# Attention, then two mixtures of experts: attention's row-max scaling and tail on other engines, weight splits placed among attention's units, acc scalings spread over product groups

## The chip, the cores and the metric

The kernel runs on one core of a Trainium2 chip. The metric is the device time of one execution in microseconds (us), lower is better. PE is the tensor engine, DVE the vector engine, ACT the scalar engine, POOL the GpSimd engine; SP only issues DMAs here. Each engine runs its own instructions strictly in order, and waits on semaphores for the others.

## The reference, cut to what matters

Sizes are B = 4, H = 8, S = 576, D = 64; N = B*S = 2304 tokens of DM = 512; E = 8 experts of hidden width F = 1024.

```
scores = where(mask, scale * q @ k.T, -1e9)     # window of 32 back; in heads 4 to 7 every 4th position
attn   = exp(scores - scores.max(-1)); attn /= attn.sum(-1) + 1e-9
x      = (attn @ v).transpose(0, 2, 1, 3).reshape(N, DM)

# first mixture: every token goes to one expert, 288 tokens at most each, best gate logits first
out[tokens of e] = relu(x[tokens of e] @ w1[e]) @ w2[e]

# second mixture: on the output of the first
P = exp(logits - logits.max())
for _ in range(8):
    P /= P.sum(1) + 1e-9;  P /= P.sum(0) + 1e-9;  P *= N / E
out = sum over e of P[:, e] * (relu(x @ w1[e]) @ w2[e])
```

## The kernel before, in words

**Attention** (L105 to L335) cuts the four batches into 25 units (`NU`), most of 96 queries of both kinds of heads (plain and dilated), and runs a software pipeline over n = 0 to 27: in step n PE makes the scores of unit n (mask and k.q products, L167, L174), DVE the row maximum (L180) and its scaling by -SC (L181, a tensor_mul of two small SBUF tiles), PE transposes the exponentials of unit n-1 (L197), DVE copies them out of PSUM (L204), ACT makes the 8 exponentials of unit n (L189), and PE multiplies unit n-2 by v (L215), with the gate logits of 128 tokens beside it where these are due (L280). DVE divides by the row sums (`rc`, `xt`, L219 to L221). `x_out` (unit n-3) splits `xt` in a float16 high part (ACT, L232) and a low part (POOL, L234), which SP stores to `xd` in DRAM (L237). The gate logits read `xd` back transposed; for the last batch `x_turn` transposes `xo` on PE (L250) into tiles of its own in PSUM, and ACT copies these into `xl` (L254); the table `TURN` says after which steps. All q and k of batches 1 to 3 are loaded ahead of the loop on SP's queue (L121), ahead of the first store to `xd`.

**Routing.** `Router.phase` (L444 to L572) finds the tokens of one expert in search steps: DVE compares (L476), PE counts (L480), DVE tests (L482), PE spreads the result (L485), DVE narrows (L488 to L490, L468). Phase 0 has nothing else to run beside it; the kernel puts dummy matmuls there (`warm`, L643), and the first six of eight pieces of expert 0's weights of the second mixture's hidden stage: `weights`, with a high half by ACT (L679) and a low half by DVE (L680), 128x1024 each. The last two pieces come in the first mixture's expert 0.

**The mixtures.** The first mixture's products are at L731 and L768, and further ones at L812. In `last()`, the end of stage 1, the Sinkhorn rounds (L1103 to L1143) run beside these as a second stream, a round at each `yield 6000` of the main stream's costs (a planner's nanoseconds); rounds that are left over run in stage 2's first block. In a round DVE divides rows and columns (L1132 to L1142) and PE sums over partitions (L1138). Stage 2 works expert by expert in blocks of tokens: `s_l1` (L995) and `s_l2` (L1033) with seven products each that are combined by additions on ACT and DVE. `add()` (L1057 to L1063) takes a finished product out of PSUM; for e = 1 it first scales two rows of the accumulator `acc` by expert 0's weight P on ACT (L1057, twice), then copies the product (L1058).

Of the kernel before, what the change touches and what calls it, by code (L numbers as in the profile page):

```python
# [16 lines left out]
OP = mybir.AluOpType  # L17
# [66 lines left out]
TURN = {NU - 1: (NU - 7, NU - 6), NU: (NU - 5, NU - 4), NU + 2: (NU - 2, NU - 1)}  # L84
# [22 lines left out]
def attention(tc, q, k, v, masks, wg, ident, xd, L, zero):  # L107

    nc = tc.nc
    with ExitStack() as ctx:  # L110
# [8 lines left out]
        def load_qk(nm, b, kind):  # L119
            x = raw[nm, b, kind] = one.tile([128, 2, S], F32, name="raw%s%d%d" % (nm, kind, b))  # L120
            nc.sync.dma_start(x, src[nm][b, :, 2 * kind:2 * kind + 2])  # L121
# [13 lines left out]
        negc = one.tile([QB, 2, 4], F32)  # L135
        nc.gpsimd.memset(negc, -SC)
# [40 lines left out]
        def row_max(u):  # L177
            p, gs = SS[u], part(u, 4)
            nm = wk.tile([QB, 2, 4], F32, name="nm")
            nc.vector.tensor_reduce(nm[:, :, gs], p[:, :, gs], axis=AX.X, op=OP.max)  # L180
            nc.vector.tensor_mul(nm[:, :, gs], nm[:, :, gs], negc[:, :, gs])  # L181
            PP[u] = nm

        def exps(u):
            p, nm, gs = SS.pop(u), PP[u], part(u, 4)
            e = wk.tile([QB, 2, 4, 128], F32, name="e")
            for s in range(2):
                for g in range(gs.start, gs.stop):
                    nc.scalar.activation(e[:, s, g, :], p[:, s, g, :], AF.Exp, bias=nm[:, s, g:g + 1], scale=SC)  # L189
            PP[u] = e  # L190
# [15 lines left out]
        def pv(u, extra):  # L206
# [4 lines left out]
            hs, ks = part(u, H), part(u, 2)  # L211
            for h in range(hs.start, hs.stop):
# [5 lines left out]
            xt = wk.tile([QB, 2, 4, D], F32, name="xt")  # L218
            nc.vector.tensor_scalar(rc[:, ks], pp[:, ks, :, D:], 1e-9 / SX, None, op0=OP.add)  # L219
            nc.vector.reciprocal(rc[:, ks], rc[:, ks])  # L220
            nc.vector.tensor_mul(xt[:, ks], pp[:, ks, :, :D], rc[:, ks].to_broadcast([QB, ks.stop - ks.start, 4, D]))  # L221
            XT[u] = xt
            for f in fin:
                f()

        def x_out(u):
            xt, ks = XT.pop(u), part(u, 2)
            if u in XO:
                xo = XO[u]
            else:  # L230
                xo = wk.tile([QB, 2, 2, 4, D], F16, name="xo")
# [10 lines left out]
        def x_turn(*units):  # L242

            for u in units:
                p = ps.tile([128, 2, 512], F32, name="ps_s").bitcast(F16)[:, :, :4 * QB].rearrange(
                    "p k (c q) -> p k c q", c=4)
                ks = part(u, 2) if u > (B - 1) * NJ else slice(1, 2)
                for kind in range(ks.start, ks.stop):
                    for c in range(4):
                        nc.tensor.transpose(p[:, kind, c, :], XO[u][:, kind, c // 2, 2 * (c % 2):2 * (c % 2) + 2, :],  # L250
                                            idh)
                for kind in range(ks.start, ks.stop):
                    for o, n, tok, st in tokens_of(QB * UNITS[u][kind][1], QB, kind):
                        nc.scalar.activation(xl[kind][:, :, tok:tok + st * (n - 1) + 1:st], p[:, kind, :, o:o + n],  # L254
                                             AF.Copy)

        XB, XO = {}, {}
# [30 lines left out]
        for b in range(1, B if True else 2):  # L288
            for kind in (1, 0):
                for nm in "kq":  # L290
                    load_qk(nm, b, kind)
            if b == 1:
                for kind in (1, 0):
                    load_v(b, kind)
        nc.scalar.activation(wgh, wgf, AF.Copy, scale=SG)
        nc.vector.scalar_tensor_tensor(wgl, wgf, SG, wgh, op0=OP.mult, op1=OP.subtract)
        xl = [one.tile([128, 4, S], F16, name="xl%d" % kind) for kind in range(2)]
        for n in range(NJ + 1):
            XO[(B - 1) * NJ + n] = one.tile([QB, 2, 2, 4, D], F16, name="xo%d" % n)
        first = S * (B - 1) // 128  # L300
        for n in range(NU + 3):
# [5 lines left out]
            if n < NU:  # L307
                exps(n)
            if n in FILL:
                warm(FILL[n])  # L310
            if n == NU + 1:
                x_turn(NU - 3)
            if 2 <= n <= NU + 1:
                pv(n - 2, [loaded.pop(0)[1] for _ in range(1 if n < NU else 2) if loaded and loaded[0][0] <= n])
# [3 lines left out]
            if n >= 3:  # L318
                x_out(n - 3)
# [9 lines left out]
            x_turn(*TURN.get(n, ()))  # L329
        p = ps.tile([128, 2, 512], F32, name="ps_v", bufs=1)  # L330
        rest = [i for _, i in loaded] + list(range(first, NT))
# [61 lines left out]
class Router:  # L393
# [39 lines left out]
    def start(self, ctx):  # L433
        self.wk = ctx.enter_context(self.tc.tile_pool(name="r_wk", bufs=2))
# [169 lines left out]
class Moe:  # L604
    def __init__(self, ctx, tc, router, xd, ident, w1a, w2a, wg2, w1b, w2b, out, ps, zero):
        nc = self.nc = tc.nc
        self.tc, self.r, self.xd, self.out, self.ps = tc, router, xd, out, ps
# [3 lines left out]
        self.big, self.raw, self.sm = pool("m_big", 1), pool("m_raw", 4), pool("m_s", 1)  # L611
# [3 lines left out]
        self.acc = self.big.tile([128, NT, DM], F32, name="acc")  # L615
# [6 lines left out]
        self.W, self.balanced, self.scattered = {}, False, []  # L622
        self.wb = [[self.big.tile([128, 4, 7, 256], F16, name="w%d%s" % (n, c)) for c in "hl"] for n in (1, 2)]
# [11 lines left out]

    def psum(self):
# [8 lines left out]
    def weights(self, key, letter, fetch, some=slice(None)):  # L645
# [9 lines left out]
        todo = todo[some]  # L655
        live, tiles = [], {lay: t for (k, lay), t in self.W.items() if k == key}
# [13 lines left out]
        for n in range(len(todo)):  # L670
            (lay, k, per, m), r = live.pop(0)
            if lay not in tiles:
                if letter == "a":
                    tiles[lay] = [self.wp.tile([128, (KT, FT)[lay], m], F16, name="w%d%s" % (lay, c)) for c in "hl"]
                else:
                    tiles[lay] = self.wflat[lay]
                self.W[key, lay] = tiles[lay]
# [337 lines left out]
    def s_l2(self, e):  # L1015
# [62 lines left out]
        for q, t, p in order:  # L1078
            yield from prod(q, t, p)
            if p[-1] == every[-1] and q in (2, 6, 4, 3):  # L1080
# [25 lines left out]
    def sinkhorn(self):  # L1106
# [24 lines left out]
        for it in range(8):  # L1131
# [4 lines left out]
            yield 6000  # L1136
# [9 lines left out]
    def stage1(self, ctx):  # L1146

        pool = lambda n, b: ctx.enter_context(self.tc.tile_pool(name=n, bufs=b))
# [13 lines left out]
        for _ in w0:  # L1162
            pass
# [6 lines left out]
        def fetched(ph):  # L1170
            w = self.weights(("a", ph), "b", self.fetch_gather(ph))
# [5 lines left out]
        first = itertools.chain(fetched(0), self.weights(("b", 0), "a", self.fetch_static(0), slice(6, None)))  # L1177

        self.ready = self.direct(1)
        def main():  # L1180
# [10 lines left out]
            for ph in range(E):  # L1191
# [34 lines left out]
        self.warm(16)  # L1226
# [65 lines left out]
def tile_kernel(ctx, tc, q, k, v, wg, w1a, w2a, wg2, w1b, w2b, masks, ident, rtab, thr, out):  # L1292
    nc = tc.nc
    with tc.manual_schedule():
# [5 lines left out]
        attention(tc, q, k, v, masks, wg, ident, xd, L, router.zero)  # L1300
        ps = ctx.enter_context(tc.tile_pool(name="ps", bufs=2, space=bass.MemoryType.PSUM))
        router.ps = ps
        moe = Moe(ctx, tc, router, xd, ident, w1a, w2a, wg2, w1b, w2b, out, ps, router.zero)
        with ExitStack() as stage:
            moe.stage1(stage)
# [21 lines left out]
```

## Time and profile before

| what | value |
|---|---|
| median of 3 runs | 1838.8 us (1835.52 to 1842.16) |
| the profiled execution | 1833.92 us, its span 1832.1 us |
| mean granted clock of PE in it | 0.979 |
| busy share of the span: PE, DVE, ACT, POOL | 96%, 75%, 46%, 12% |

All times of rows are microseconds from the span's start, in that one execution; it lies 4.9 us below the median of the runs. PE's busy share is an average: attention takes 0 to 128 us, phase 0 of the routing to 165 us, the first mixture and the Sinkhorn rounds to 652 us, stage 2 the rest.

### The profile page before, as it was taken

To read this page: it belongs to the slowest core of one execution; us is meant where nothing else is said; L and a number is where in the kernel's file an instruction comes from. 1 tells how busy PE (TensorE), PEld (TensorE's weight loads), DVE (VectorE), ACT (ScalarE), POOL (GpSimd) and SP (SyncE) were. 2 spreads that over 40 slices of the span, in tenths; PEclk is the share of its full clock that TensorE was granted. 3 is DMA by queue.
4 is the path that set the end of the run, shared out by engine and by line. 5 is a ranking of instruction groups with operands and counts; after the bars stand their busy time and mean duration, and the time that the engine had idled before them with its cause. 6 is when DMAs were issued, how large, how long until landed. Compare 5 with 4: busy or idle time off the path is not lost.

```text
span 1832.1 us, 35300 instructions
## 1 busy us (share of the span) xinstructions
PE 1752.7 (96%) x14518; PEld 1297.8 (71%) x14518; DVE 1371.9 (75%) x2625; ACT 839.1 (46%) x1502; POOL 227.4 (12%) x284
## 2 busy tenths in 40 slices
PE   8986899999999889999999999999999999999998
PEld 6873666666677647766777777777777777777776
DVE  5877776686744767877887888788878878887656
ACT  4662333333344344564444555444555444554333
POOL 1224222233221000000000000000000000000111
PEclk8988899999999999999999999999999999999999
DMA  8554323343242314433244432444352353433120
GB/s 304 148 138 138 110 83 95 109 119 104 88 142 83 122 47 156 147 131 146 112 167 164 184 125 105 171 156 152 136 195 93 127 213 140 163 122 141 55 96 35
DMA packets 106161, 241.19 MB, mean 132 GB/s; under 512 B 46704, under 2 KB 70512, under 8 KB 99088
## 3 DMA queue, kind: packets, MB, share of 16 engines
q1 hardware_dynamic: 84736, 151.34, 23.9%
q0 software_dynamic: 20592, 87.53, 13.4%
q8 instruction: 113, 1.85, 0.4%
q14 instruction: 48, 0.39, 0.1%
q10 hardware_dynamic: 672, 0.08, 0.0%
HBM read 173.83 MB, written 61.73 MB: 129 GB/s over the span
## 4 chain that ended last, share of the span: by engine, by line
PE 70%; DVE 11%; issue 10%; ACT 4%; DMA 3%; POOL 1%; SPq 0%; POOLq 0%; ACTq 0%; DVEq 0%
PE mm L995 26%; PE mm L1033 22%; PE mm L731 8%; PE mm L812 5%; PE mm L768 2%; PE ps_v L215 1%; PE r L480 1%; PE ps_p L197 1%; DVE hl L952 1%; PE ps_s L174 1%; POOL out_dram L1047 1%; DVE w1l L680 1%; DMA wgf<-in_wg_dram 1%; DMA rawk<-in_k_dram 1%; DVE G L552 1%
## 5 line engine op out<-in xcount | busy, mean ns | idle before, releaser
L995 PE MATMUL mm<-xb,w1h 128*128 128x384 f16 x2352 | 574.6, 327 | 5.3 <-DVE mm L966 4.9
L1033 PE MATMUL mm<-w2h,hh 128*128 128x256 f16 x1764 | 480.8, 273 | 8.5 <-DVE t L1059 4.4
L1033 PE MATMUL mm<-w2h,hl 128*128 128x256 f16 x1764 | 480.8, 273 | 0.0
L1033 PE MATMUL mm<-w2l,hh 128*128 128x256 f16 x1764 | 480.8, 273 | 0.0
L995 PE MATMUL mm<-xb,w1l 128*128 128x384 f16 x1176 | 383.9, 326 | 0.0
L1033 PEld LDWEIGHTS <-hh 128*128 128x128 f16 x3528 | 345.2, 98 | 52.6 <-issue 10.6
L995 PEld LDWEIGHTS <-w1h 128*128 128x128 f16 x2352 | 230.4, 98 | 159.5 <-issue 11.6
L1033 PEld LDWEIGHTS <-hl 128*128 128x128 f16 x1764 | 172.6, 98 | 20.0
L952 DVE TENSOR_TENSOR hl<-r,hh 128x1536 f16<-128x1536 f32 x84 | 147.5, 1756 | 41.2 <-ACT hh L951 41.2
L995 PEld LDWEIGHTS <-w1l 128*128 128x128 f16 x1176 | 115.2, 98 | 76.5 <-issue 0.7
L947 ACT ACTIVATE r<-mm 128x384 f32<-128x384 f32 x252 | 119.0, 481 | 98.3 <-PE mm L995 98.3
L951 ACT ACTIVATE hh<-r 128x1536 f16<-128x1536 f32 x84 | 124.6, 1483 | 46.4 <-DVE r L976 44.4
L913 POOL DMA_DIRECT2D ws<-raw x48 | 26.0, 541 | 941.1 <-ACT raw L864 673.6
L958 ACT ACTIVATE mm<-mm 128x384 f32<-128x384 f32 x84 | 40.3, 479 | 180.8 <-PE mm L995 180.8
L952 DVE TENSOR_TENSOR hl<-S,hh 128x1152 f16<-128x1152 f32 x84 | 113.6, 1352 | 0.0
L731 PE MATMUL mm<-xt,w1h 128*128 128x288 f16 x512 | 97.2, 289 | 1.4 <-ACT xt L745 1.4
L1043 DVE SCALAR_TENSOR_TENSOR acc<-t,P,acc 128x512 f32<-128x512 f32 x126 | 94.8, 752 | 4.5
L951 ACT ACTIVATE hh<-S 128x1152 f16<-128x1152 f32 x84 | 96.4, 1147 | 0.0
L864 ACT ACTIVATE raw<-raw 128x1024 f16<-128x1024 f32 x48 | 50.6, 1055 | 96.6 <-DVE raw L849 47.7
L734 ACT ACTIVATE w1h<-mm 128x288 f16<-128x288 f32 (+1 forms) x120 | 47.1, 397 | 102.6 <-PE mm L731 100.5
L735 DVE SCALAR_TENSOR_TENSOR w1l<-mm,w1h 128x288 f16<-128x288 f32 (+1 forms) x120 | 50.7, 435 | 55.1 <-ACT w1h L734 54.5
L731 PE MATMUL mm<-x2l,w0h 128*128 128x256 f16 x288 | 81.1, 282 | 6.8 <-DVE x2l L773 6.8
(258 smaller groups left out, 2972.1 us busy)
## 6 DMA issues: line engine op xcount, KB each, us to landing
xb<-xw SPq DMA_DIRECT2D x30, 1344.0 KB, 5.6
ws<-raw POOLq DMA_DIRECT2D x48, 448.0 KB, 2.7
ws<-r POOLq DMA_DIRECT2D x48, 448.0 KB, 3.0
raw<-in_w2b_dram SPq DMA_DIRECT2D x32, 512.0 KB, 9.4
raw<-in_w1b_dram SPq DMA_DIRECT2D x56, 256.0 KB, 6.3
w1h<-ws SPq DMA_DIRECT2D x6, 1792.0 KB, 7.5
w1l<-ws SPq DMA_DIRECT2D x6, 1792.0 KB
w2h<-ws SPq DMA_DIRECT2D x6, 1792.0 KB
```

Of the source, the lines that this page charges most:

```text
L731: nc.tensor.matmul(p, a[:, k, 128 * f:128 * (f + 1)], rhs(k, b), start=(k == 0 and i == 0), stop=(k == KT - 1 and i == 2))
L734: nc.scalar.activation(h[0][:, f, :n], p, AF.Relu)
L735: nc.vector.scalar_tensor_tensor(h[1][:, f, :n], p, 0.0, h[0][:, f, :n], op0=OP.max, op1=OP.subtract)
L812: nc.tensor.matmul(p, a[:, f, c], b[:, f, :], start=(f == 0 and n == 0), stop=(f == FT - 1 and n == 2))
L864: self.nc.scalar.activation(hi[:, k], x, AF.Copy, scale=sw)
L947: nc.scalar.activation(o, p, AF.Relu, scale=SH)
L951: yield nc.scalar.activation(hq[0][:, i, k], x, AF.Copy)
L952: yield V.tensor_sub(hq[1][:, i, k], x, hq[0][:, i, k])
L958: nc.scalar.activation(Q[i], P[i], AF.Copy)
L995: nc.tensor.matmul(p, w[u][:, 2 * j + i // 2, k, 128 * (i % 2):128 * (i % 2 + 1)], x[:, v, r, j], start=(q in (1, 5) and j == 0 and n == 0 ...
L1033: nc.tensor.matmul(p, h[u][:, i, a, 128 * t:128 * (t + 1)], w[v][:, i, b, :], start=(q in (1, 7) and i == 0 and j == 0), stop=(q in (2, 3) ...
L1043: V.scalar_tensor_tensor(self.acc[:, r, :], x, self.P[:, r, e:e + 1], self.acc[:, r, :], op0=OP.mult, op1=OP.add)
```

## The change

1. The scaling of the row maximum goes from DVE to ACT.
2. `exps` is cut in two halves of four exponentials, and `x_out` of unit n-3 stands between them.
3. `x_turn` transposes float32 `xt` (two transposes a kind where there were four) into free columns of the PSUM tile that `pv` uses in the same step, for units 18 to 22 in steps 21 to 25, for 23 and 24 after the loop. The high part is an ACT copy as before, in pieces half as wide; the low part is a DVE subtraction out of PSUM.
4. q and k of batches 2 and 3 are loaded in steps 6, 7, 12 and 13.
5. All eight pieces of expert 0's second-mixture weights are split inside attention: 16 halves of 128x512, one on ACT and the one before on DVE in each of the steps 6 to 23; their loads are issued from step 4 on.
6. Phase 0 has no splits; its `warm` counts go from 5 to 3 per step, and the one ahead of the first mixture from 16 to 6.
7. In `s_l2` for e = 1 the six `acc` scalings stand one after each fourth product group.
8. Sinkhorn's `yield 6000` becomes `yield 4000`: all eight rounds fall into `last()`.

```diff
             nm = wk.tile([QB, 2, 4], F32, name="nm")
             nc.vector.tensor_reduce(nm[:, :, gs], p[:, :, gs], axis=AX.X, op=OP.max)
-            nc.vector.tensor_mul(nm[:, :, gs], nm[:, :, gs], negc[:, :, gs])
+            nc.scalar.activation(nm[:, :, gs], nm[:, :, gs], AF.Copy, scale=-SC)
...
-        def x_turn(*units):
...
+        def x_turn(u, p):
+
+            p = p[:, :, 264:264 + 2 * QB].rearrange("p k (c q) -> p k c q", c=2)
+            ks = part(u, 2) if u > (B - 1) * NJ else slice(1, 2)
+            for kind in range(ks.start, ks.stop):
+                for c in range(2):
+                    nc.tensor.transpose(p[:, kind, c, :], XT[u][:, kind, 2 * c:2 * c + 2, :], idf[:QB, :QB])
...
+            for n, (o, i, x) in enumerate(parts):
+                if x == 0:
+                    nc.scalar.activation(o, i, AF.Copy)
+                else:
+                    nc.vector.tensor_sub(o, i, hi[n - len(hi)])
...
-            if n < NU:
-                exps(n)
+            ex = exps(n) if n < NU else iter(())
+            next(ex, None)
+            if 3 <= n <= NU:
+                x_out(n - 3)
+            for _ in ex:
+                pass
...
+            if 4 <= n:
+                next(side, None)
...
+            b, c = divmod(n - NJ, NJ)
+            if 0 <= b < B - 2 and c < 2:
+                for nm in "kq":
+                    load_qk(nm, b + 2, 1 - c)
...
+    def first_weights(self, ctx):
...
+            for c in (slice(0, 512), slice(512, 1024)):
+                nc.scalar.activation(hi[:, c], r[:, c], AF.Copy, scale=(SW1, SW2)[lay])
+                yield
+                nc.vector.scalar_tensor_tensor(lo[:, c], r[:, c], (SW1, SW2)[lay], hi[:, c], op0=OP.mult,
+                                               op1=OP.subtract)
+                if c.stop == 1024 and n + 4 < len(todo):
+                    load(n + 4)
...
             if q == 2:
-                for r in (row(t, 0), row(t, 1)) if e == 1 else ():
-                    nc.scalar.activation(self.acc[:, r, :], self.acc[:, r, :], AF.Copy, scale=self.P[:, r, 0:1])
...
+            if n % 4 == 3 and rows:
+                r = rows.pop(0)
+                nc.scalar.activation(self.acc[:, r, :], self.acc[:, r, :], AF.Copy, scale=self.P[:, r, 0:1])
...
-            yield 6000
+            yield 4000
...
-            self.warm(1 if need < 2000 else 5)
-            if i % 2 and i < 14:
-                next(w0, None)
+            self.warm(1 if need < 2000 else 3)
...
-        self.warm(16)
+        self.warm(6)
```

First place: DVE in one of attention's steps with gate logits. `nm` is the row maximum, `pt` the transposed exponentials, `xt` the output of a unit, `L` the gate logits; `w0l` is a low half of the weights. Before:

```order
L180 TENSOR_REDUCE nm<-ps_s 96x8
L181 TENSOR_TENSOR nm<-nm,negc 96x8
L204 COPY pt<-ps_p 128x768
L219 TENSOR_SCALAR rc<-ps_v 96x8
L220 RECIPROCAL rc<-rc 96x8
L221 TENSOR_TENSOR xt<-ps_v,rc 96x512
L282 COPY L<-ps_v 128x8
```

and after:

```order
L176 TENSOR_REDUCE nm<-ps_s 96x8
L201 COPY pt<-ps_p 128x768
L218 TENSOR_SCALAR rc<-ps_v 96x8
L219 RECIPROCAL rc<-rc 96x8
L220 TENSOR_TENSOR xt<-ps_v,rc 96x512
L274 COPY L<-ps_v 128x8
L669 SCALAR_TENSOR_TENSOR w0l<-raw,w0h 128x512
```

The scaling is gone from its place behind the maximum, and a split, which reads two SBUF tiles as the scaling did, stands at the step's end, right ahead of the next maximum.

Second place: ACT, and then DVE, in step 23 of the changed kernel, near attention's end. `xl_186` and `xl_187` are the transposed outputs of the last batch, `e` the exponentials, `xo` the high part that is stored.

```order
L177 ACTIVATE nm<-nm 96x8
L186 ACTIVATE e<-ps_s,nm 96x128 x4
L228 ACTIVATE xo<-xt 96x2x256
L186 ACTIVATE e<-ps_s,nm 96x128 x4
L251 ACTIVATE xl_186<-ps_v 128x2x96
L251 ACTIVATE xl_187<-ps_v 128x2x96
```

```order
L176 TENSOR_REDUCE nm<-ps_s 96x8
L201 COPY pt<-ps_p 128x768
L253 TENSOR_TENSOR xl_186<-ps_v,xl_186 128x2x96
L253 TENSOR_TENSOR xl_187<-ps_v,xl_187 128x2x96
L218 TENSOR_SCALAR rc<-ps_v 96x8
L219 RECIPROCAL rc<-rc 96x8
L220 TENSOR_TENSOR xt<-ps_v,rc 96x512
```

Before, these steps held no L253 on DVE and ACT's copies into `xl` stood behind the exponentials of unit 24; now the subtractions stand ahead of the division of the same step, behind ACT's copies, which stand behind all eight exponentials.

Third place: ACT in stage 2's first block with e = 1, behind the hidden layer. `raw` are weights being prepared for the next expert, `t_9009` and its like take the products out of PSUM. Before:

```order
L864 ACTIVATE raw<-raw 128x1024
L864 ACTIVATE raw<-S 128x768
L1057 ACTIVATE acc<-acc,P 128x512 x2
L1058 ACTIVATE t_9033<-mm 128x256
L1057 ACTIVATE acc<-acc,P 128x512 x2
L1058 ACTIVATE t_9037<-mm 128x256
L1057 ACTIVATE acc<-acc,P 128x512 x2
L1058 ACTIVATE t_9041<-mm 128x256
```

and after:

```order
L1115 ACTIVATE acc<-acc,P 128x512 x2
L898 ACTIVATE raw<-raw 128x1024
L898 ACTIVATE raw<-S 128x768
L1115 ACTIVATE acc<-acc,P 128x512 x3
L898 ACTIVATE raw<-raw 128x1024
L898 ACTIVATE raw<-S 128x768
L1115 ACTIVATE acc<-acc,P 128x512
L1090 ACTIVATE t_9009<-mm 128x256
L1090 ACTIVATE t_9013<-mm 128x256
L1090 ACTIVATE t_9017<-mm 128x256
```

All six scalings now stand ahead of the first copy out of PSUM.

## Rows read from the trace of the kernel before

**Rows 1.** The page, busy time and share of the span.

```profile
PE 1752.7 (96%) x14518; PEld 1297.8 (71%) x14518; DVE 1371.9 (75%) x2625; ACT 839.1 (46%) x1502; POOL 227.4 (12%) x284
```

**Rows 2.** Stretches: length, busy PE, PEld, DVE, ACT, POOL; clock, DMA share, GB/s.

```profile
60.00:80.00 20.00, 20.00 (x257) 17.76 (x256) 19.13 (x33) 13.16 (x46) 5.77 (x5) 1.00 0.58 141
...
600.00:640.00 40.00, 34.57 (x278) 25.87 (x275) 30.58 (x86) 14.55 (x34) 0.00 (x0) 0.91 0.38 114
```

**Rows 3.** Timeline of PE, 36 to 56 us: start, duration, instruction, idle before.

```profile
36.92 1.12 PE L174 MATMUL ps_s<-rawk,rawq 64*96 64x128 f32 x16
40.41 2.20 PE L197 MATMUL ps_p<-idf,e 96*128 96x96 f32 x8 [2.37 <-ACT e L189]
...
45.90 2.03 PE L174 MATMUL ps_s<-rawk,rawq 64*96 64x128 f32 x16
...
51.53 1.12 PE L174 MATMUL ps_s<-rawk,rawq 64*96 64x128 f32 x16
...
55.16 1.01 PE L174 MATMUL ps_s<-rawk,rawq 64*96 64x128 f32 x14
```

**Rows 4.** Timeline of ACT: at 39 us, and in a later step.

```profile
39.47 0.63 ACT L232 ACTIVATE xo<-xt 96x512 f16<-96x512 f32 x1 [4.62 <-DMA xd<-xo]
...
106.69 2.15 ACT L189 ACTIVATE e<-ps_s,nm 96x128 f32<-96x128 f32 x8 [1.37 <-DVE nm L181]
```

**Rows 5.** Timeline of DVE: L181 at 54 us, and a step with gate logits.

```profile
53.95 0.16 DVE L181 TENSOR_TENSOR nm<-nm,negc 96x8 f32<-96x8 f32 x1
...
104.50 1.21 DVE L180 TENSOR_REDUCE nm<-ps_s 96x8 f32<-96x1024 f32 x1
105.75 0.83 DVE L181 TENSOR_TENSOR nm<-nm,negc 96x8 f32<-96x8 f32 x1
106.50 0.94 DVE L204 COPY pt<-ps_p 128x768 f32<-128x768 f32 x1
...
108.53 1.21 DVE L180 TENSOR_REDUCE nm<-ps_s 96x8 f32<-96x1024 f32 x1
```

**Rows 6.** Timeline of POOL in the same step.

```profile
105.40 1.15 POOL L234 TENSOR_TENSOR xo<-xt,xo 96x512 f16<-96x512 f32 x1 [2.88 <-ACT xo L232]
```

**Rows 7.** Timeline of DVE: a search step without a split, one with.

```profile
132.39 0.27 DVE L482 TENSOR_SCALAR ok<-r,rem 8x64 f16<-8x64 f32 x1 [0.77 <-PE r L480]
132.94 0.23 DVE L488 TENSOR_SCALAR pen<-r 128x64 f32<-128x64 f32 x1 [0.27 <-PE r L485]
...
139.03 0.24 DVE L482 TENSOR_SCALAR ok<-r,rem 8x32 f16<-8x32 f32 x1 [0.47 <-PE r L480]
139.20 1.20 DVE L680 SCALAR_TENSOR_TENSOR w0l<-raw,w0h 128x1024 f16<-128x1024 f32 x1
140.33 0.17 DVE L488 TENSOR_SCALAR pen<-r 128x32 f32<-128x32 f32 x1
```

**Rows 8.** Timeline of PE ahead of the first mixture.

```profile
165.58 5.62 PE L643 MATMUL mm<-zero 128*128 128x512 f16 x16
```

**Rows 9.** Waits of PE from 610 us to the end: us, times, longest.

```profile
PE mm L995 <- DVE mm L966: 4.9, 3, 2.4
PE mm L1033 <- DVE t L1059: 4.4, 3, 2.7
PE mm L1033 <- DVE t L1063: 4.0, 3, 1.3
```

**Rows 10.** Timeline of ACT in stage 2's first block with e = 1.

```profile
704.83 1.32 ACT L1057 ACTIVATE acc<-acc,P 128x512 f32<-128x512 f32 x2
706.05 0.36 ACT L1058 ACTIVATE t<-mm 128x256 f32<-128x256 f32 x1
```

**Rows 11.** Timeline of DVE between Sinkhorn rounds.

```profile
624.66 2.09 DVE L867 SCALAR_TENSOR_TENSOR w1l<-raw,w1h 128x1024 f16<-128x1024 f32 x2
...
647.05 0.31 DVE L1139 TENSOR_REDUCE cs<-r 128x8 f32<-128x144 f32 x1 [2.43 <-PE r L1138]
...
649.03 0.31 DVE L1135 TENSOR_TENSOR P<-P,rs 128x144 f32<-128x144 f32 x1
```

More of the change, by code (lines that the diff above doesn't have):

```diff
@@ L1 @@
-import itertools
 from contextlib import ExitStack
@@ L104, in lay_v, with attention @@
     return out
-def attention(tc, q, k, v, masks, wg, ident, xd, L, zero):
+def attention(tc, q, k, v, masks, wg, ident, xd, L, zero, side):
     nc = tc.nc
@@ L119, in load_qk @@
         def load_qk(nm, b, kind):
-            x = raw[nm, b, kind] = one.tile([128, 2, S], F32, name="raw%s%d%d" % (nm, kind, b))
+            x = raw[nm, b, kind] = ld.tile([128, 2, S], F32, name="raw%s%d" % (nm, kind))
             nc.sync.dma_start(x, src[nm][b, :, 2 * kind:2 * kind + 2])
@@ L226, in x_out @@
         def x_out(u):
[L227 to L231, printed above, removed]
+            xt, ks = XT[u], part(u, 2)
+            xo = wk.tile([QB, 2, 2, 4, D], F16, name="xo", bufs=4)
             nc.scalar.activation(xo[:, ks, 0], xt[:, ks], AF.Copy)
@@ L240, in x_out @@
                         xo[p0:p0 + n, kind].rearrange("q a h d -> q (a h d)"))
-        def x_turn(*units):
[L244 to L257, printed above, removed]
+        def x_turn(u, p):
[4 more added lines that the diff above has]
+                    nc.tensor.transpose(p[:, kind, c, :], XT[u][:, kind, 2 * c:2 * c + 2, :], idf[:QB, :QB])
+            parts = [(xl[kind][:, x, :, tok:tok + st * (n - 1) + 1:st], p[:, kind, :, o:o + n], x)
+                     for x in range(2) for kind in range(ks.start, ks.stop)
+                     for o, n, tok, st in tokens_of(QB * UNITS[u][kind][1], QB, kind)]
+            hi = [o for o, _, x in parts if x == 0]
+            for n, (o, i, x) in enumerate(parts):
[3 more added lines that the diff above has]
+                    nc.vector.tensor_sub(o, i, hi[n - len(hi)])
+        XB = {}
         def x_load(c, c1):
@@ L287, in attention @@
         loaded = []
[L288 to L294, printed above, removed]
+        for kind in (1, 0):
+            for nm in "kq":
+                load_qk(nm, 1, kind)
+        for kind in (1, 0):
+            load_v(1, kind)
         nc.scalar.activation(wgh, wgf, AF.Copy, scale=SG)
         nc.vector.scalar_tensor_tensor(wgl, wgf, SG, wgh, op0=OP.mult, op1=OP.subtract)
-        xl = [one.tile([128, 4, S], F16, name="xl%d" % kind) for kind in range(2)]
-        for n in range(NJ + 1):
-            XO[(B - 1) * NJ + n] = one.tile([QB, 2, 2, 4, D], F16, name="xo%d" % n)
+        xl = [one.tile([128, 2, 2, S], F16, name="xl%d" % kind) for kind in range(2)]
         first = S * (B - 1) // 128
-        for n in range(NU + 3):
+        for n in range(NU + 2):
             if n < NU:
@@ L328, in attention @@
                 x_load(first, first + 1)
-            x_turn(*TURN.get(n, ()))
+            if n == NU:
+                loaded += [(n, i) for i in (first, first + 1)]
+        x_turn(NU - 2, ps.tile([128, 2, 512], F32, name="ps_s"))
+        x_turn(NU - 1, ps.tile([128, 2, 512], F32, name="ps_p", bufs=1))
+        x_out(NU - 2)
+        x_out(NU - 1)
         p = ps.tile([128, 2, 512], F32, name="ps_v", bufs=1)
-        rest = [i for _, i in loaded] + list(range(first, NT))
+        rest = [i for _, i in loaded] + list(range(first + 2, NT))
         o = p[:, 0, :E * len(rest)].rearrange("p (n e) -> p n e", e=E)
@@ L433, in start @@
     def start(self, ctx):
-        self.wk = ctx.enter_context(self.tc.tile_pool(name="r_wk", bufs=2))
+        self.wk = ctx.enter_context(self.tc.tile_pool(name="r_wk", bufs=2, side="right"))
     def psum(self):
@@ L622, in __init__, with after_attention @@
         self.W, self.balanced, self.scattered = {}, False, []
+    def after_attention(self, ctx):
+        pool = self.tc.tile_pool(name="ps", bufs=2, space=bass.MemoryType.PSUM)
+        self.ps = self.r.ps = ctx.enter_context(pool)
+        self.big = ctx.enter_context(self.tc.tile_pool(name="m_big", bufs=1))
+        self.acc = self.big.tile([128, NT, DM], F32, name="acc")
         self.wb = [[self.big.tile([128, 4, 7, 256], F16, name="w%d%s" % (n, c)) for c in "hl"] for n in (1, 2)]
@@ L654, in weights @@
                 todo.append((lay, k, per, m))
-        todo = todo[some]
-        live, tiles = [], {lay: t for (k, lay), t in self.W.items() if k == key}
+        live, tiles = [], {}
         def load(it):
@@ L672, in weights @@
             if lay not in tiles:
[L673 to L677, printed above, removed]
+                self.W[key, lay] = tiles[lay] = self.wflat[lay]
             hi, lo = (t[:, k:k + per, :] for t in tiles[lay])
@@ L1077, in s_l2 @@
         order += [(q, t, every) for q in (6, 4, 3) for t in ts]
-        for q, t, p in order:
+        rows = [row(t, half) for t in ts for half in range(2)] if e == 1 else []
+        for n, (q, t, p) in enumerate(order):
             yield from prod(q, t, p)
+            if n % 4 == 3 and rows:
+                r = rows.pop(0)
+                nc.scalar.activation(self.acc[:, r, :], self.acc[:, r, :], AF.Copy, scale=self.P[:, r, 0:1])
             if p[-1] == every[-1] and q in (2, 6, 4, 3):
@@ L1175, in fetched @@
             return w
-        first = itertools.chain(fetched(0), self.weights(("b", 0), "a", self.fetch_static(0), slice(6, None)))
+        first = fetched(0)
         self.ready = self.direct(1)
@@ L1299, in tile_kernel @@
         router = Router(ctx, tc, L, rtab, thr, ("r", 2))
[L1300 to L1303, printed above, removed]
+        moe = Moe(ctx, tc, router, xd, ident, w1a, w2a, wg2, w1b, w2b, out, router.zero)
         with ExitStack() as stage:
+            attention(tc, q, k, v, masks, wg, ident, xd, L, router.zero, moe.first_weights(stage))
+            moe.after_attention(ctx)
             moe.stage1(stage)
```

82 lines of the change are left out of this document (46 added, 36 removed).

## The prediction

> **What bounds the kernel now.** I start with the page's busy shares: PE works 96% of the span, every other engine 75% or less [rows 1]. So a saving counts only where PE waits, runs at half clock, or idles behind another engine. The table by stretches shows where that is. Attention's middle has no idle PE, yet DVE is full too, 19.13 of 20 us [rows 2]: a step ends when the slower of the two is through. The Sinkhorn stretch (PE 34.57 of 40, clock 0.91) has slack on PE. Then the timelines of these and of attention's edges.
>
> Early in attention PE stands for 2.37 us on ACT's exponentials, and its next scores take 2.03 us where the same 16 matmuls take 1.12 before and after [rows 3]: TensorE is at its lower level, 1.2 GHz, in place of 2.4. ACT was late because it waited 4.62 us for an earlier store of `xo` [rows 4]; in the code that store stands on SP's queue behind all loads of q and k.
>
> A step late in attention takes 108.53 - 104.50 = 4.03 us, and DVE has not a gap in it. The scaling L181 takes 0.83 us there and 0.16 us elsewhere, for the same 96x8 [rows 5]; in the slow case POOL's subtraction runs from 105.40 to 106.55, and L181 ends 0.03 us after it [rows 6]. A DVE instruction on two SBUF tiles is evidently held while POOL reads. In stage 2 the list of waits leaves 4.9 us on the hidden layer and 4.4 + 4.0 us on products whose PSUM is late [rows 9].
>
> **The change part by part.** The sum is against the profiled execution, 1833.9 us.
>
> Early attention: -7. Two steps take 51.53 - 36.92 = 14.6 us. The next, undisturbed and without gate logits, takes 55.16 - 51.53 = 3.63 [rows 3]. Two such are 7.3, so 7.3 us are lost. With eight q and k loads out of the way and `xo` in four buffers the store is issued earlier, and the halved exponentials don't stand behind it. The weight pieces now loaded at the same time are smaller than what goes. Bounds: -2.4 (only the wait goes, the clock falls anyway) and -7.3.
>
> Steps 7 to 22: +5. DVE loses the 0.75 us from L181's start to the next [rows 5], and gets a split of 512 columns: half of 1.20 us [rows 7], 0.6. Alone that is 3.28 + 0.62 = 3.9 us against 4.03, a gain of 0.1 a step, or 1 to 2 in all. But the split reads two SBUF tiles too. Counted from the maximum's start, DVE comes to it at 4.03 - 0.75 = 3.28 in a step with gate logits, 0.07 earlier without. POOL's subtraction starts after the maximum (1.21), the scaling on ACT (no row; between 0.16, as on DVE [rows 5], and 0.36 for ACT's 256 columns [rows 10]; I take 0.25), half of 2.15 for four exponentials, 0.63 for `xo` [rows 4], and some 0.1 for each of the two hand-overs: 3.3 to 3.4. That is a dead heat. Where POOL is first, the split waits until 3.3 + 1.15 = 4.45 and the step lasts 5.05, 1.0 more than before. Eight of the sixteen steps have gate logits, and in those PE has the logits' matmuls to do ahead of DVE's division, so DVE tends to be late there. Five steps lost is my value; bounds -2 (none) and +10 (eight, and two of the others).
>
> By the Trainium skill ("SBUF — State Buffer", "Who interferes with whom") a DVE instruction with two SBUF inputs contends with a GpSimd instruction that reads SBUF, and the one issued first holds the shared pair while the other fully blocks. The trace's 0.16 against 0.83 agrees. By it, the steps cost nothing if the split is always issued first and the total would be 5 to 7 lower; POOL first everywhere would make it 5 higher.
>
> Steps 22 to 25: +6. Here one chain runs through all engines within a step: maximum 1.25, hand-over and scaling 0.35, four exponentials 1.07, `xo` 0.63, four more 1.07, ACT's two copies into `xl` (192 columns each; 256 take 0.36 [rows 10], so 0.3 to 0.35 each, 0.65), the last subtraction on DVE (192 columns out of PSUM, between 0.2 and half of the 0.94 of 768 columns [rows 5], say 0.35), then division and multiplication, as from the end of L204, 107.44, to the next maximum, 108.53 [rows 5]: 1.1. That is 6.5 against 4.03. Two steps pay 2.4 and the one ahead, with one kind only, about half: 6. After the last scores the work is other but no shorter: fewer transposes (float32 ones), two subtractions more; I count it even. Bounds +2 (the maximum of the next step is not held, since DVE's slack of the steps before absorbs it) and +9 (PE falls to its lower level in the gaps that the chain leaves, as at 46 us, where the scores took 0.9 us more [rows 3], and three steps pay that).
>
> Routing, phase 0: -5. A search step's DVE stretch from L482 to L488 takes 140.33 - 139.03 = 1.30 us with a split and 132.94 - 132.39 = 0.55 without [rows 7]. Nothing else is there for PE, so each split lies on the path. Six of them give 6 x 0.75 = 4.5, or 6 x 1.2 = 7.2 where nothing at all covers one; I take 5. The lower bound is 3, if with fewer dummy matmuls PE's sums run more at the lower level.
>
> Ahead of the first mixture: -3. The 16 dummy matmuls take 5.62 us [rows 8]; ten fewer free 3.5 us, of which I take 1.7, as the gathers of tokens and weights behind them may not be in. Two splits of 1.2 us leave expert 0's first mixture, where PE follows DVE part of the time: 1.3 of 2.4.
>
> `acc` scalings: -7.5. A pair, 1.32 us, stands ahead of each copy out of PSUM [rows 10], and PE then waits 2.7 and 1.3 us per block, 8.4 in three blocks [rows 9]. Now all six are done when the first product ends; while seven products a tile run, ACT has the time. Bounds -5 and -8.4.
>
> Sinkhorn: -1. Three rounds leave stage 2's first block, where PE waits 4.9 us [rows 9], all of it to gain at best. They go into a stretch where DVE already works 30.58 of 40 us [rows 2], at 2.3 us each (647.05 to 649.34) among splits of 2.09 a pair [rows 11]. A round's sum on PE then stands in PE's queue until DVE is through; I walk that to four stalls of 0.5 to 1.1, 3.8 in all. Bounds -5 and +4.
>
> The identity's load and POOL's conversion of it, now at the start, have no row there; nothing, or as much as POOL's larger subtraction (1.15 [rows 6]) if the masks wait behind it. I take nothing, since other loads are in flight then.
>
> Sum: -7 + 5 + 6 - 5 - 3 - 7.5 - 1 = -12.5, so 1821 us for such an execution. The runs' median lies 4.9 us above the profiled one; from it, 1838.8 - 12.5 = 1826.
>
> **Rivals.**
> No lock: DVE always reaches its split first. For it: 3.28 against 3.3 or more. The steps give -1 in place of +5: 1820. From a scaling of 0.3 us on ACT on it is the likelier.
>
> Lock and tail at their upper bounds: POOL first in ten steps (+5 more), the tail at the lower clock (+3). For it: L181, which came 0.35 us after POOL's start, was held [rows 5, 6]. 1834; with the early clock not back, 4.6 more: 1838, which is no difference.
>
> The wrong side: Sinkhorn's spacing below what DVE can do. If, in each of the five rounds that move or come closer, PE waits for a pair of splits and the round, 2.09 + 2.3, the rounds cost 22 in place of gaining 1: 1849. It decides from 18 us, 3.6 a round, where the time passes 1844.3. Against it: PE has queued matmuls ahead of each sum, and the round at 647 waited for PE, not PE for it [rows 11].
>
> The spread of the scalings does nothing, since ACT's conversions of `raw` now between them hold the copies as well: 7.5 back, 1833.
>
> **How the numbers follow.** Forecast (1821 to 1831) 0.45; no lock 0.22 (1812 to 1821); upper bounds, or scalings that bring nothing, 0.24 (1831 to 1839, half of it still below 1833.3); the slower side 0.06, several terms failing at once 0.03. The range from 1812 to 1838 leaves out 0.2: the slower side, the best of no lock, the worst of the upper bounds. A measurement tells 0.3%, 5.5 us, from no change: faster (below 1833.3) 0.79, same 0.13, slower 0.08.
>
> **What would show it.** Right: no wait of PE on ACT near 40 us; steps of 3.9 and of 5 us mixed between 55 and 105, the split of 512 columns at 0.6 us in some and up to 1.75 in others beside POOL's subtraction; steps of 6 us or more around 22 to 24; L482 to L488 near 0.55 throughout phase 0; no wait on L1059's and L1063's successors; small waits on the Sinkhorn sums. Wrong: splits at 0.6 throughout, a half-clock stretch in a place that I don't name, or PE waits of over 2 us in the Sinkhorn stretch.

## The result, and the profile after

The change made the kernel slower: 1853.83 us median (1849.83 to 1856.87, 5 runs) against 1842.16 of the kernel before in five runs beside it (the 1838.8 above is the median of the first three), ratio 1.0077 [1.0063, 1.0090]. The forecast was 1826, faster. The profiled execution has a span of 1852.0 us, 19.9 above that of before, while the medians differ by 11.7; e10 below tells which part of the 19.9 does not come back. Five marks in the two traces say where it arises:

| stretch | before | after | difference |
|---|---|---|---|
| start to the scores of unit 21 | 99.1 | 94.3 | -4.8 |
| to the copy of the last logits (L335) | 28.9 | 57.5 | +28.7 |
| to the first mixture's first product | 45.8 | 38.5 | -7.4 |
| to stage 2's first product | 479.5 | 489.7 | +10.3 |
| stage 2 | 1178.8 | 1172.0 | -6.8 |

The largest part, more than the whole loss, lies in attention's last steps. PE's timeline there (start, duration, instruction, idle before):

```profile
94.31 1.12 PE L170 MATMUL ps_s<-rawk,rawq 64*96 64x128 f32 x16
95.36 0.93 PE L194 MATMUL ps_p<-idf,e 96*128 96x96 f32 x8
96.12 0.33 PE L244 MATMUL ps_v<-idf,xt 96*128 96x96 f32 x2
102.05 2.82 PE L214 MATMUL ps_v<-rawv,pt 128*96 128x65 f32 x16 [5.60 <-DVE xl L253]
...
106.03 2.02 PE L170 MATMUL ps_s<-rawk,rawq 64*96 64x128 f32 x16
...
117.88 2.02 PE L170 MATMUL ps_s<-rawk,rawq 64*96 64x128 f32 x16
```

ACT, and then DVE, in the same step:

```profile
99.76 1.13 ACT L186 ACTIVATE e<-ps_s,nm 96x128 f32<-96x128 f32 x4
100.76 0.62 ACT L251 ACTIVATE xl<-ps_v 128x192 f16<-128x192 f32 x1
```

```profile
96.74 1.21 DVE L176 TENSOR_REDUCE nm<-ps_s 96x8 f32<-96x1024 f32 x1
...
101.41 0.58 DVE L253 TENSOR_TENSOR xl<-ps_v,xl 128x192 f16<-128x192 f32 x1 [2.59 <-ACT xl L251]
105.21 0.16 DVE L218 TENSOR_SCALAR rc<-ps_v 96x8 f32<-96x8 f32 x1 [3.22 <-PE ps_v L272]
...
108.10 1.22 DVE L176 TENSOR_REDUCE nm<-ps_s 96x8 f32<-96x1024 f32 x1 [1.04 <-PE ps_s L170]
```

The turn's transposes (L244) stand ahead of pv (L214) in PE's order and in pv's own tile, `ps_v`. pv then waits 5.60 us, until 0.06 us after DVE's subtraction (L253) has read them. That subtraction waits for ACT's copy, this for eight exponentials, these for the maximum at 96.74. Behind pv stand the logits and the next scores, and only these let the next maximum begin, at 108.10. So the chain closes over PE as well: 5.3 us from the maximum to the subtraction's end, then 6.1 us of pv, logits and scores. Three such steps (from one unit's scores to the next's) take 11.7, 11.9 and 11.4 us where a step of before took 4.03 [rows 5]. PE's list of waits to 240 us, and the table of stretches (columns as in rows 2), have the sums: 17.6 us of waiting in five waits, and a mean granted clock of 0.67, between the two levels, and then of 0.50, wholly at the lower one.

```profile
PE ps_v L214 <- DVE xl L253: 17.6, 5, 5.6
```

```profile
90.00:125.00 35.00, 22.14 (x206) 19.49 (x204) 17.83 (x33) 16.72 (x56) 6.67 (x5) 0.67 0.26 62
125.00:152.00 27.00, 20.61 (x224) 18.67 (x225) 10.85 (x34) 5.95 (x17) 2.30 (x2) 0.50 0.19 47
```

The Trainium skill ("PSUM — Partial Sum Buffer", "PSUM bank collisions raise a hardware error") says that two engines may not touch one PSUM bank within the same 32 partitions at the same time, even at different addresses, and that the compiler's scheduler adds a dependency between them. The trace has such a dependency, pv writes columns that the subtraction does not read and waits for it, but it goes by the whole tile. In the first of these steps the turn has one kind only: its transposes at 96.12 fill columns of the second half of `ps_v`, pv's first products go to the first half, and they wait the 5.60 us all the same. e9 below gives the turn another tile.

The rest of the profile. Early in attention PE's wait on ACT near 40 us [rows 3] is gone, and the scores of units 8 and 9, at 45.90 and 51.53 before, start sooner:

```profile
41.67 1.12 PE L170 MATMUL ps_s<-rawk,rawq 64*96 64x128 f32 x16
...
45.30 1.12 PE L170 MATMUL ps_s<-rawk,rawq 64*96 64x128 f32 x16
```

In the steps between there are splits (L669) of 0.68 us and three of 1.69 to 1.70, with POOL's subtraction much longer where the split is not. DVE, then POOL:

```profile
65.59 0.68 DVE L669 SCALAR_TENSOR_TENSOR w0l<-raw,w0h 128x512 f16<-128x512 f32 x1
69.54 1.69 DVE L669 SCALAR_TENSOR_TENSOR w0l<-raw,w0h 128x512 f16<-128x512 f32 x1
```

```profile
65.14 2.15 POOL L230 TENSOR_TENSOR xo<-xt,xo 96x512 f16<-96x512 f32 x1 [2.11 <-ACT xo L228]
69.40 1.28 POOL L230 TENSOR_TENSOR xo<-xt,xo 96x512 f16<-96x512 f32 x1 [2.11 <-ACT xo L228]
```

In phase 0 DVE gets from L482 to L488 in 0.50 us, against 1.30 beside a split [rows 7]:

```profile
161.89 0.24 DVE L482 TENSOR_SCALAR ok<-r,rem 8x32 f16<-8x32 f32 x1 [0.47 <-PE r L480]
162.39 0.19 DVE L488 TENSOR_SCALAR pen<-r 128x32 f32<-128x32 f32 x1 [0.26 <-PE r L485]
```

PE's waits from 594 us on (L1029, L1067 and L1174 are L995, L1033 and L1138 of before): stage 2's fall from 13.3 us [rows 9] to the 3.3 and 2.1 shown and 0.4 more, and the sums of the Sinkhorn rounds wait 2.5.

```profile
PE mm L1029 <- DVE mm L1000: 3.3, 3, 2.2
...
PE r L1174 <- DVE P L1171: 2.5, 3, 1.8
PE mm L1067 <- DVE t L1091: 2.1, 1, 2.1
```

### The profile page after: what moved, and what is told of

The parts are those of the page before. It is cut to its first block, busy times and chain, and to the rows that moved or that the text cites. A ratio compares the mean times of both kernels' runs of the same rounds, so it can differ in the third digit from the quotient of the medians.

```text
span 1852.0 us, 35253 instructions
## 1 busy us (share of the span) xinstructions
PE 1760.2 (95%) x14470; PEld 1304.8 (70%) x14470; DVE 1367.6 (74%) x2623; ACT 841.1 (45%) x1535; POOL 234.9 (13%) x283
## 3 DMA queue, kind: packets, MB, share of 16 engines
q0 software_dynamic: 20592, 87.53, 13.3%
## 4 chain that ended last, share of the span: by engine, by line
PE 71%; DVE 11%; issue 10%; ACT 5%; DMA 1%; POOL 1%; POOLq 0%; SPq 0%; DVEq 0%; ACTq 0%
PE mm L1029 25%; PE mm L1067 23%; PE mm L765 8%; PE mm L846 5%; PE ps_v L214 2%; PE mm L802 2%; DVE hl L986 1%; PE ps_s L170 1%; PE r L480 1%; PE ps_p L194 1%; POOL out_dram L1081 1%; DVE w1l L714 1%; ACT w1h L713 1%; DVE G L476 1%; ACT raw L898 1%
## 5 line engine op out<-in xcount | busy, mean ns | idle before, releaser
L1029 PE MATMUL mm<-xb,w1h 128*128 128x384 f16 x2352 | 574.6, 327 | 4.2 <-DVE mm L1000 3.3
L1067 PE MATMUL mm<-w2h,hh 128*128 128x256 f16 x1764 | 480.8, 273 | 2.3 <-DVE t L1091 2.1
L1067 PE MATMUL mm<-w2h,hl 128*128 128x256 f16 x1764 | 480.8, 273 | 0.0
L1067 PE MATMUL mm<-w2l,hh 128*128 128x256 f16 x1764 | 480.8, 273 | 0.0
L1029 PE MATMUL mm<-xb,w1l 128*128 128x384 f16 x1176 | 384.0, 326 | 0.0
L1067 PEld LDWEIGHTS <-hh 128*128 128x128 f16 x3528 | 345.2, 98 | 44.9 <-issue 2.8
L1029 PEld LDWEIGHTS <-w1h 128*128 128x128 f16 x2352 | 230.3, 98 | 159.2 <-issue 11.4
L1067 PEld LDWEIGHTS <-hl 128*128 128x128 f16 x1764 | 172.6, 98 | 20.0
L1029 PEld LDWEIGHTS <-w1l 128*128 128x128 f16 x1176 | 115.2, 98 | 76.5 <-issue 0.7
L769 DVE SCALAR_TENSOR_TENSOR w1l<-mm,w1h 128x288 f16<-128x288 f32 (+1 forms) x120 | 50.5, 435 | 55.1 <-ACT w1h L768 52.7
```

The costliest lines, as they stand in the source:

```text
L769: nc.vector.scalar_tensor_tensor(h[1][:, f, :n], p, 0.0, h[0][:, f, :n], op0=OP.max, op1=OP.subtract)
L1029: nc.tensor.matmul(p, w[u][:, 2 * j + i // 2, k, 128 * (i % 2):128 * (i % 2 + 1)], x[:, v, r, j], start=(q in (1, 5) and j == 0 and n == 0 ...
L1067: nc.tensor.matmul(p, h[u][:, i, a, 128 * t:128 * (t + 1)], w[v][:, i, b, :], start=(q in (1, 7) and i == 0 and j == 0), stop=(q in (2, 3) ...
```

## The experiments

Each result is the ratio to the kernel before in runs on the same chip, with its 95% interval, and then the median in us; between runs on different chips only ratios are compared. "Tail" is the time from unit 21's scores to the copy of the last logits in the profiled execution: 28.9 before, 57.5 after. "Steps" are the three in it that end with the scores of units 22, 23 and 24.

**e1**, the turn behind pv in the same tile.

```diff
-            if turn is not None:
-                x_turn(turn, p)
             for h in range(hs.start, hs.stop):
...
+            if turn is not None:
+                x_turn(turn, p)
             fin = [logits(p[:, 0, 480
```

> The changed kernel, but x_turn's transposes, copies and subtractions stand behind pv's matmuls of the same PSUM tile, not ahead of them. Theory A (PE's order: pv waits until DVE has read the turned values out of its own tile, so that pv, the logits and the next scores stand in one chain with the maximum, the exponentials, the copies and the subtractions): no wait of L214 on L253 is left, the steps 22 to 24 fall from 12 us to the 6.5 to 7.5 that ACT and DVE need alone, from the last full step's scores to the end of attention some 35 us in place of 57.5, the whole 1829 to 1836. Rival B (ACT and DVE's chain with the copies and subtractions is by itself what takes the time, PE's wait is its shadow): the steps stay over 10 us, the whole at 1846 or more. Rival C (the lower clock is the cause, the wait only its beginning): the steps fall by 3 us each, the whole 1841 to 1846.

1.0016 [1.0005, 1.0026], 1840.14; tail 48.1, steps of 8.1 to 9.3. This is none of the theories: the steps fall by 2.1 to 3.6 us, in size nearest to rival C, whose cause, the clock, this run does not separate. pv's wait is gone, but the logits, in the same tile, wait in its place, which the expectation had overlooked. PE's waits:

```profile
PE ps_v L272 <- DVE xl L253: 9.7, 5, 3.1
PE ps_v L212 <- DVE xt L220: 2.3, 1, 2.3
```

**e2**, as e1, copies and subtractions behind the division and the logits' copy.

```diff
+            if turn is not None:
+                x_turn(turn, p, "put")
             fin = [logits(p[:, 0, 480
...
             for f in fin:
                 f()
+            if turn is not None:
+                x_turn(turn, p, "get")
```

> As e1, and the copies and subtractions stand behind the division of the step too. Theory A: the division is no longer held by ACT's copies, steps of 5.5 to 6.5 us, the whole 1 to 4 us below e1. Rival B: over 10 us a step, 1846 or more. Rival D (in e1 the division isn't on the path): the same as e1 within 1 us.

0.9954 [0.9937, 0.9970], 1829.31; tail 38.1, steps of 4.2, 8.2 and 5.2. This has theory A's direction, but is 11 us below e1 and not 1 to 4: of the three steps' own PE work nothing waits any more, only the next pv does (4.8 us in three waits).

**e3**, the turn as before, all else of the change kept: `x_turn`, `TURN`, `left`, the `xo` tiles and the loop's end of the kernel before.

```diff
+TURN = {NU - 1: (NU - 7, NU - 6), NU: (NU - 5, NU - 4), NU + 2: (NU - 2, NU - 1)}
...
-        def x_turn(u, p):
+        def x_turn(*units):
```

> The changed kernel with the turn of the kernel before (float16 transposes of xo into a ps_s tile of their own, two units after a step, copies by ACT alone), every other part of the change kept. Theory A (the new turn is what made the kernel slower, all else together gains): attention ends 28 to 34 us sooner than in the changed kernel, the whole 1820 to 1827, so faster than before. Rival E (the other parts lose as much as they gain): 1838 to 1846, no faster than before.

0.9926 [0.9909, 0.9942], 1824.3: theory A. Without the new turn the change makes the kernel faster, so the turn is what made it slower. Attention's end comes 23.8 us sooner than in the changed kernel, less than the 28 to 34 expected: the tail is 33.7, and PE is almost wholly at the lower clock in its last part (0.52 from 110 to 129).

**e9**, the changed kernel, its turn in a tile of its own, nothing moved.

```diff
-                x_turn(turn, p)
+                x_turn(turn, ps.tile([128, 2, 512], F32, name="ps_s"))
```

> The changed kernel with one thing different: the turn's transposes go to a PSUM tile of their own (one of the two that the scores use), at the same place in every engine's order. Theory A' (pv waits because it writes the banks that DVE and ACT still read, not because of where the turn stands in the order): no wait of pv on the subtractions, 6 to 7.5 us a step in place of 12, since the scores must now wait for their second buffer; the whole 15 to 24 us below the changed kernel. Rival B' (PE's order or the chain of ACT and DVE is the cause, whatever the tile): the steps stay over 10 us, the whole within 8 us.

0.9964 [0.9948, 0.9980], 1827.67, against 1845.08 of the changed kernel beside it (e10), 17.4 us less; tail 39.9, steps of 7.6, 6.8 and 7.2. Theory A': with the same order on every engine pv no longer waits for the subtraction, and the scores wait for their buffer instead, as expected. PE:

```profile
96.08 0.33 PE L244 MATMUL ps_s<-idf,xt 96*128 96x96 f32 x2
96.25 1.50 PE L214 MATMUL ps_v<-rawv,pt 128*96 128x65 f32 x16
100.90 1.01 PE L163 MATMUL ps_s<-mk,idb 96*96 96x256 bf16 x4 [2.87 <-ACT e L186]
```

What holds the maximum at 111.30 is then DVE itself, behind the subtraction, the division and a split:

```profile
103.91 1.22 DVE L176 TENSOR_REDUCE nm<-ps_s 96x8 f32<-96x1024 f32 x1 [0.25 <-PE ps_s L170]
...
108.81 0.85 DVE L253 TENSOR_TENSOR xl<-ps_s,xl 128x192 f16<-128x192 f32 x3 [2.48 <-ACT xl L251]
...
110.70 0.68 DVE L669 SCALAR_TENSOR_TENSOR w1l<-raw,w1h 128x512 f16<-128x512 f32 x1
111.30 1.21 DVE L176 TENSOR_REDUCE nm<-ps_s 96x8 f32<-96x1024 f32 x1
```

e9 changes the tile, and with it the clock (0.83 from 90 to 110, 0.63 to 135); how the 17.4 us divide between the wait and the clock it doesn't tell.

**e8**, dummy matmuls in pv's wait.

```diff
                 x_turn(turn, p)
+                fill = ps.tile([128, 2, 512], F32, name="ps_s")
+                for _ in range(12):
+                    nc.tensor.matmul(fill[:, 0, :], zero[:, :128], zero, start=True, stop=True)
```

> The changed kernel with 12 dummy matmuls between the turn's transposes and pv in the five steps, which fill PE's wait (they change no output). Theory A with a price of the clock (the chain is the wait, and the lower clock adds pv's and the scores' doubling, some 3 us a step): the granted clock stays near 1.0, the steps 22 to 24 fall from 12 to 8.5 to 9.5, the whole 1840 to 1846. Rival L (the clock adds nothing on this chain, or PE's dummies stand in it): 11 us a step or more, 1852 or more.

1.0037 [1.0023, 1.0051], 1840.52; tail 52.7, steps of 11.7, 10.5 and 10.2. Inconclusive on the price of the clock: in these steps the 12 matmuls took 2.75 us of the wait, the rest (3.05, 1.72 and 1.87 us) still passed idle, and the clock was 0.78 to 0.84 in stretches of 20 us. In the second step and the third pv ran at the upper level, the scores behind it not:

```profile
112.52 1.57 PE L217 MATMUL ps_v<-rawv,pt 128*96 128x65 f32 x16 [1.72 <-DVE xl L256]
...
115.19 2.03 PE L170 MATMUL ps_s<-rawk,rawq 64*96 64x128 f32 x16
```

**e10**, the changed kernel again.

> The changed kernel itself beside the others. Steady: 0.5 to 1.0% slower than before; the stretch of experts 1 to 6 of the first mixture, 338 us in its first profile against 334 to 335 in all other kernels, at 334 to 336 if that was chance, at 338 again if it belongs to the change.

1.0062 [1.0042, 1.0081], 1845.08; tail 57.5 again, with 17.4 us of pv's waits. This profile's span is 10.6 us above that of before, not 19.9. Experts 1 to 6 took 334.9 us, 338.0 in the first profile and 334.4 before, so nearly all of that difference was chance. Expert 0 took 62.8, against 64.2 before and 65.9 in the first profile, so its difference isn't told either. Of the first table's +10.3 only +4.1 is left, with +5.0 behind expert 6's first output (85.9 against 80.9), where the Sinkhorn rounds run.

**e4**, Sinkhorn at 6000 in the changed kernel, and **e6**, the same in e3.

```diff
-            yield 4000
+            yield 6000
```

> The changed kernel with the Sinkhorn rounds at 6000 as before. Theory F (the denser rounds cost PE in stage 1's end about what they give back in stage 2's first block): the first block of stage 2 begins 4 to 5 us sooner, then loses 3 to 5 in its waits, the whole within 2 us of the changed kernel, 1852 to 1856. Rival G (the forecast: more given back than lost): 1 to 7 us slower, 1855 to 1861.

> e3 with the Sinkhorn rounds at 6000. Theory F' (as e4 has it: the denser rounds lose 4.5 in stage 1's end and give 1 back): 2.5 to 4.5 us below e3, 1819 to 1823, with no wait of over 0.3 us on a round's sum. Rival G' (they pay): 1825 or more.

e4: 1.0045 [1.0031, 1.0059], 1845.62, but its runs spread from 1843 to 1853 and its interval overlaps that of e10, so the whole decides nothing. e6: 0.9905 [0.9889, 0.9922], 1816.83, against e3's 0.9926 [0.9909, 0.9942]; these overlap as well, and what decides is a stretch of the profiles. From expert 6's first output to stage 2 it is 80.9 before, 85.8 after, 85.5 in e3, 81.5 in e4, 80.9 in e6, and over all profiles 84.8 to 85.9 with the rounds at 4000 (eight) and 80.9 to 81.9 at 6000 (six, before among them). Stage 2 takes 1172.0 after, 1172.0 in e3, 1173.1 in e4 and 1171.2 in e6; but the seven profiles at 4000 with the scalings spread range from 1169.7 to 1172.3, so a gain of about 1 us there isn't told from chance. The denser rounds cost 4.3 to 4.6 us (in e3 against e6, 2.2 of it are waits of PE on their sums), and no clear gain stands against that. Theory F's cost is borne out, the 3 to 5 us that stage 2 was to lose at 6000 are not; theory F' has it right.

**e5**, e3 with the `acc` scalings in `add()` again, and out of the product groups.

```diff
             if q == 2:
+                for r in (row(t, 0), row(t, 1)) if e == 1 else ():
+                    nc.scalar.activation(self.acc[:, r, :], self.acc[:, r, :], AF.Copy, scale=self.P[:, r, 0:1])
```

> e3 with the six acc scalings back in front of the copies out of PSUM. Theory H (the spread alone brings stage 2's gain): PE waits again for the two additions, 7 to 9 us in three blocks, stage 2 lasts 5 to 8 us longer than in e3, the whole 1829 to 1833. Rival I (the gain of stage 2 is that of the Sinkhorn rounds that left its first block): less than 2 us longer, 1823 to 1827.

0.9962 [0.9948, 0.9976], 1828.09, stage 2 5.3 us longer than e3's (5.0 to 7.7 longer than in the seven profiles above): theory H. PE's waits there, 7.0 us:

```profile
PE mm L1073 <- DVE t L1099: 4.4, 3, 2.7
...
PE mm L1073 <- DVE t L1103: 2.6, 2, 1.3
```

**e7**, e6 with the split right behind the maximum.

```diff
                 row_max(n)
+            if 7 <= n < NU:
+                next(side, None)
...
                 if c.stop == 1024 and n + 4 < len(todo):
                     load(n + 4)
+                yield
```

> e6 with DVE's split of each step right behind the maximum, where POOL does not run, in place of the step's end. Theory J (DVE and POOL hold each other when a DVE instruction reads two SBUF tiles): no split over 0.75 us, POOL's subtraction back to 1.15 from 1.3 to 2.1, no step of 5 us, 2 to 5 us less until the last scores; and since the clock fell behind such a step in e3, up to 4 less behind them: the whole 1814 to 1820. Rival K (the split costs its 0.6 us anywhere, and a later copy of the transposes holds PE instead): within 1.5 us of e6.

0.9889 [0.9872, 0.9905], 1813.58, against e6's 0.9905; the intervals overlap, but the profile is theory J's. No step of 5 us is left, no split takes over 0.69 us, the tail is 28.9 against e6's 30.7, and the last logits come at 120.9 against 124.2. By groups of instructions to 110 us (count | busy us, mean ns), e6 first, then e7:

```profile
L232 POOL TENSOR_TENSOR xo<-xt,xo 96x512 f16<-96x512 f32 (+1 forms) x21 | 31.6, 1504 | 73.8 <-ACT xo L230 49.1 <-DVE xt L219 22.6 <-DMA rawq<-in_q_dram 2.1
L675 DVE SCALAR_TENSOR_TENSOR w1l<-raw,w1h 128x512 f16<-128x512 f32 x8 | 7.4, 930 | 0.0
```

```profile
L232 POOL TENSOR_TENSOR xo<-xt,xo 96x512 f16<-96x512 f32 (+1 forms) x23 | 26.1, 1135 | 81.3 <-ACT xo L230 69.9 <-DVE xt L219 3.2 <-DMA xd<-xo 2.8
L677 DVE SCALAR_TENSOR_TENSOR w1l<-raw,w1h 128x512 f16<-128x512 f32 x8 | 5.4, 677 | 0.0
```

**e11**, e7 with the scaling of the maximum on DVE, by a constant tile as before.

```diff
-            nc.scalar.activation(nm[:, :, gs], nm[:, :, gs], AF.Copy, scale=-SC)
+            nc.vector.tensor_mul(nm[:, :, gs], nm[:, :, gs], negc[:, :, gs])
```

> e7 with the scaling of the row maximum back on DVE. Theory J (what cost 0.75 us a step before was POOL's subtraction beside it, and with x_out between the halves of the exponentials the subtraction no longer falls there): the scaling takes 0.16 us in every step, the whole within 2 us of e7. Rival (the move to ACT itself is worth its 0.75 us): the scaling takes 0.5 us or more, 3 to 9 us slower.

0.9894 [0.9867, 0.9921], 1814.2, and the scaling takes 0.16 us all 25 times (ns: least, median, most):

```profile
L180 DVE TENSOR_TENSOR nm<-nm,negc x25: 159/161/168, 14.5 to 107.1; 96x8 f32<-96x8 f32 x23, 96x4 f32<-96x4 f32 x2
```

Theory J: the move to ACT was not needed; what took 0.83 us [rows 5] was POOL's subtraction beside it [rows 6].

**e12**, e7 with two buffers for `xo`.

```diff
-                xo = wk.tile([QB, 2, 2, 4, D], F16, name="xo", bufs=4)
+                xo = wk.tile([QB, 2, 2, 4, D], F16, name="xo")
```

> e7 with two buffers for xo in place of four. Theory M (the early stall of before came from the loads of q and k ahead of the stores on SP's queue): no wait of ACT on a store over 1 us in the first 60 us, the whole within 2 us of e7. Rival N (the two more buffers cure it): the wait and the half clock near 40 us are back, 5 to 8 us slower.

0.9889 [0.9862, 0.9915], 1814.34, as e7. ACT waits 1.6 us on a store, over theory M's bound of 1, against 4.62 before [rows 4]; the clock from 38 to 46 us is 1.00 where it was 0.62 before, and the whole doesn't show the wait. So rival N is out, and that the loads ahead of the stores were the cause is borne out so far; a changed kernel with all loads ahead of the loop was not tried.

## Why the prediction was wrong, point by point

- **Early attention, -7.** Right: unit 9's scores start at 45.3 against 51.5, although the first start 0.8 later.
- **Steps 7 to 22, +5.** The mechanism was right, the size too large: three held splits, not five, and from unit 9's scores to unit 21's +1.4.
- **Steps 22 to 25, +6: the step that failed.** "Here one chain runs through all engines within a step", it said, and then summed ACT and DVE alone to 6.5 us. The sum has the division right behind the last subtraction, as if pv's products were there by then. But the diff hands `x_turn` pv's own tile, so that pv, the logits and the next scores stand in that chain too: 11.4 to 11.9 us a step, +28.7 in all, above the bound of +9. Of these, 23.1 arise in the three steps and 5.6 behind the last scores, which were counted even. With the tile changed and nothing else (e9) the steps take 6.8 to 7.6, near the sum of ACT and DVE, which had left out the split of 0.68 and put the subtraction at 0.35 where it takes up to 0.85. Even so e9's tail is 11.0 above before, since all three steps pay about 3 us, so the term was also too small without the wait. None of the rivals had this wait; the one on the slower side named Sinkhorn. How much of the 28.7 is the lower clock stays open (e8, e9).
- **Routing, -5, and ahead of the first mixture, -1.7 of the -3.** Right: -7.4 together. The late splits' -1.3, in expert 0, isn't told from chance (e10).
- **`acc` scalings, -7.5.** Right: 5.3 by e5, 5.0 to 7.7 beside the other profiles.
- **Sinkhorn, -1.** Wrong sign: +3 to +5 by e3, e4 and e6. The stalls on PE were seen (2.5 us against the 3.8 walked), the gain in stage 2's first block was hardly there: of its 4.9 us of waits 3.3 stayed, so the hidden layer waits on DVE without the rounds too. Where the other 2 us of the cost of 4.3 to 4.6 arise stays open.

With the new turn taken out (e3) the ratio is 0.9926, and the forecast, 1826 of 1838.8, stands for 0.993. That the two agree is partly luck: e3's tail costs 4.8 us, at the lower clock, where the sum has 6 for a chain that e3 doesn't have, and the Sinkhorn rounds' loss is offset by splits that cost less than summed.

## What to carry to other kernels

Before a result is put into free columns of another product's PSUM tile, list who reads it there and what else PE writes to that tile: here the products waited for those readers, in the other half of the tile too, and PE, in order, made the next steps wait as well. A cheap small instruction that seems slow may only be held by a neighbour; here the place of POOL's subtraction, not the engine of the scaling, was what mattered (e7, e11). A stream that is packed denser in one stage to free another must be priced in both (e3 against e6): the first paid 4.6 us, the second gave nothing that can be told.

## What the runs showed of the hardware that was not expected

POOL is held by DVE as well: its subtraction took 1.28 to 2.15 us beside a split where it takes 1.15 alone, and the recorded starts don't tell which side wins: at 65.14 POOL began 0.45 us ahead and was held, at 69.40 0.14 us ahead and held the split. And dummy matmuls that fill part of a wait did not keep TensorE's clock up: with 1.7 us of the wait left, the next scores still took 2.03 us in place of 1.12; in the two steps behind unit 24's scores, where the dummies left pv nothing to wait for, pv took 1.50 us in place of 2.82 (e8).
